# Attention's fixed order: new costs in its planner, four buffers for output halves, a split addition

## The chip, the cores and the metric

The kernel runs on one core of a Trainium2 chip. The metric is the device time of one execution in microseconds. Engines go by these names: PE is TensorE (matmuls and transposes), PEld its weight loads, DVE is VectorE, ACT is ScalarE, POOL is GpSimd, SP issues the DMAs. L12 is line 12 of the kernel before.

## The reference, cut to what matters

Three layers run one after the other: attention with queries pooled in pairs, a gated expert layer, and an expert layer with eight experts whose routing weights are normalised in eight rounds. Only attention's order is touched.

```python
q_pool = q.reshape(B, H, S // 2, 2, D).mean(axis=3)          # (2, 8, 576, 64)
scores = scale * np.matmul(q_pool, k.transpose(0, 1, 3, 2))  # (2, 8, 576, 1152)
scores = scores - np.max(scores, axis=-1, keepdims=True)
attn = np.exp(scores)
attn = attn / (np.sum(attn, axis=-1, keepdims=True) + 1e-09)
x = np.matmul(attn, v)                # then (1152, 512): tokens x heads * D
x = moe(x)                            # sigmoid(x @ w_gate) * (x @ w_val) @ w_out
out = moe2(x)                         # 8 experts, relu, weighted by P
```

## The kernel before, in words

**Attention.** The 16 heads are taken as eight pairs. A pair has nine units of up to 128 query rows: unit 0 holds the last 64 rows of both heads, units 1 to 4 are the other rows of the first head, 5 to 8 those of the second. Numbers are split in a high and a low part, so that a product is made of several fast ones.

For a unit `u`, PE computes the scores in three pieces (`scores`, L327/L328 for unit 0, L333/L334 for the others): columns 0 to 671 into the two banks of buffer A, columns 672 to 1151 into buffer B. There is one A and one B. DVE takes the negated maximum of A (`max_a`, step `ma`, L342) and of B (`max_b`, `mb`, L354) and the smaller of the two (`max_ab`, `m`, L360, one column). ACT takes the exponential of A with A's own maximum (`exp_a`, `ea`, L348; this frees A), that of B with the common one (`exp_b`, `eb`, L363; this frees B), and the factor between the two (`exp_ab`, `e`, L370). POOL multiplies A's part by this factor (`bring`, `b`, L374). PE transposes the unit in three groups (`turn_p`, `tpp`, L382) into PSUM buffers of kind "g", of which there are five. ACT copies the high part out (`p_high`, `ph`, L398) and DVE subtracts for the low part (`p_low`, `pl`, L402).

The product with the values runs in halves: for each head `j`, half `n` = 0 covers 256 rows, `n` = 1 covers 320. A half is 18 matmuls (`values`, `pv`, L421) into one "g" buffer. Its sums of exponentials are put together on POOL (`total`, `r1` and `r2`, L434). DVE adds 1e-9 (L439) and takes the reciprocal (L440), both in the step `r`, `reciprocals`; a half has two columns of sums, the half (0, 1) has three, since unit 0 is added. PE spreads the reciprocals (`turn_r`, `tr`, L445). ACT copies one part of the half out (`v_one`, `o1`, L457) into a buffer of kind "sw", DVE adds the other part (`o2`, L461) and multiplies by the reciprocals (`o3`, L466, L469), and POOL splits the result (`xh` at L71, `xl` at L477) into the input of the next layer. After `xl` the "sw" buffer is free; there are two.

Keys, queries and values of the next pairs are loaded by SP and prepared beside this (POOL: L71, L292, L262, L312; PE: L266, L296; ACT: L273, L302; DVE: L277).

**The planner.** Every such piece of work is a step with an engine, a due time `when`, an occupancy `takes` of its engine, a time `lasts` until its result is there (both in ns), the steps that it needs, and the buffers that it takes and frees. `arrange()` puts all steps in one order before the kernel is built. It keeps the time at which each engine is free, and again and again picks the step with the earliest possible start among those whose needs are placed and whose due time is at most `AHEAD` = 4 units past the oldest step not begun. A step on another engine than its producer may start `lasts + wake` after the producer's start, one on the same engine `takes` after it. On the chip each engine then runs its instructions in this order, each waiting for its real inputs.

**Behind attention.** The first expert layer's weights are split by `split_doubles` (L107 to L120). The first of these run on the same engine queues among the last steps of attention, by a rule of priority and not by the planner. The layer's matmuls are L712 to L714.

Of the kernel before, what the change touches and what calls it, by code (L numbers as in the profile page):

```python
# [8 lines left out]
F32 = mybir.dt.float32  # L9
# [20 lines left out]
def moe_stack_kernel(ctx: ExitStack, tc: tile.TileContext, q, k, v, wg1, wv1, wo1, wg2, w1, w2, out):  # L30
# [100 lines left out]
    with ExitStack() as pa:  # L131
# [6 lines left out]
        def slots(pool, n, shape, dt, name):  # L138
            return [pool.tile(shape, dt, tag=f"{name}{k}", name=f"{name}_{k}") for k in range(n)]
# [20 lines left out]

            "sum": slots(pw, 2, [P, 4, U], F32, "sum"),
            "rem": slots(pw, 1, [P, NJ, P], F32, "rem"),
            "sw": slots(pw, 2, [P, HALF[1][1]], F32, "sw"),
            "A": slots(ps_s, 1, [P, 2, 512], F32, "psA"),
            "B": slots(ps_s, 1, [P, 512], F32, "psB"),
            "g": slots(ps_s, 5, [P, 512], F32, "psg"),
# [2 lines left out]
        have = {}  # L169
        steps = {}  # L170

        def step(name, eng, when, takes, lasts, emit, deps=(), takes_buf=(), frees=()):


            steps[name] = dict(
                name=name, eng=eng, when=when, takes=takes, lasts=lasts, emit=emit, deps=deps, gets=takes_buf,
                frees=frees, seq=len(steps),
            )

        def arrange():  # L180

            wake = dict(PE=53, ACT=34, DVE=34, POOL=97, SP=100)
            users, need, ready = {}, {}, {e: [] for e in wake}
            for s in steps.values():
                need[s["name"]] = len(s["deps"])
                s["at"] = 0.0
                for d in s["deps"]:
                    users.setdefault(d, []).append(s)
                if not s["deps"]:
                    ready[s["eng"]].append(s)  # L190
            idle = {kind: [(0.0, k) for k in range(len(t))] for kind, t in stock.items()}
            line = sorted(steps.values(), key=lambda s: (s["when"], s["seq"]))
            turn = {kind: [s["name"] for s in line if any(k == kind for k, _ in s["gets"])] for kind in stock}
            given, front, free, out = {}, 0, dict.fromkeys(wake, 0.0), []
            begun = set()
            while len(out) < len(steps):
                while line[front]["name"] in begun or line[front]["eng"] == "SP":
                    front += 1
                limit, best = line[front]["when"] + AHEAD, None
                for eng, queue in ready.items():  # L200
                    for s in queue:
                        if s["when"] > limit and eng != "SP":
                            continue
                        t = max(free[eng], s["at"])
                        for kind, _ in s["gets"]:
                            if not idle[kind] or (kind != "g" and turn[kind][0] != s["name"]):
                                break
                            t = max(t, min(idle[kind])[0] + wake[eng])
                        else:
                            key = t, s["when"], s["seq"]  # L210
                            if best is None or key < best[0]:
                                best = key, s
                (t, _, _), s = best
                ready[s["eng"]].remove(s)
                begun.add(s["name"])
                free[s["eng"]] = t + s["takes"]
                for kind, what in s["gets"]:
                    slot = min(idle[kind])
                    idle[kind].remove(slot)
                    if kind != "g":  # L220
                        turn[kind].pop(0)
                    given[what] = kind, slot[1]
                s["got"] = [(what, *given[what]) for _, what in s["gets"]]
                for what in s["frees"]:
                    kind, k = given[what]
                    idle[kind].append((t + s["lasts"], k))
                for u in users.get(s["name"], ()):
                    own = s["takes"] if u["eng"] == s["eng"] else s["lasts"] + wake[u["eng"]]
                    u["at"] = max(u["at"], t + own)
                    need[u["name"]] -= 1  # L230
                    if not need[u["name"]]:
                        ready[u["eng"]].append(u)
                out.append((t, len(out), s))
            return [s for _, _, s in sorted(out, key=lambda x: x[:2])]
# [118 lines left out]
        def max_b(i, u):  # L353
            nc.vector.tensor_reduce(  # L354
                out=have["nm", i, u][:, 1:2], in_=have["B", i, u][:, 0:S - CA], axis=AX.X, op=ALU.max, negate=True
            )
# [54 lines left out]
        def rem_high(i, j):  # L411
            src, hi, _ = rem_parts(i, j)
            pool_copy(hi, src)
# [12 lines left out]
        def columns(j, n):  # L426
            c0 = 5 * j + 2 * n
            return slice(c0, c0 + 2 + (j == 0 and n == 1))
# [6 lines left out]

        def reciprocals(i, j, n):

            rs = have["sum", i][:, 3, columns(j, n)]
            nc.vector.tensor_scalar(out=rs, in0=rs, scalar1=eps, scalar2=None, op0=ALU.add)  # L439
            nc.vector.reciprocal(out=rs, in_=rs)  # L440

        def turn_r(i, j, n):
# [34 lines left out]
            nc.gpsimd.tensor_tensor(out=lo, in0=sw, in1=f(hi), op=ALU.subtract)  # L477

        def mm(w):
            return w / 2.4 + 13.4  # L480

        for i in range(B * NP):
            t0 = U * i
# [46 lines left out]
            for j in range(2):  # L530
# [9 lines left out]
                for g in range(3):  # L540
# [19 lines left out]
                )  # L560
                t = t0 + 4.5 + 4 * j
                step(
                    ("rh", i, j), "POOL", t, 637, 672, lambda i=i, j=j: rem_high(i, j),
                    [("rem", i, g) for g in range(3)] + [("ph", i, 3 + 4 * j, 0)],
                )
                step(
# [4 lines left out]
            for u in range(U):  # L571
                tu = t0 + order.index(u)
                js = (0, 1) if u == 0 else ((u - 1) // QT,)
                for g in range(3):
# [15 lines left out]
                )  # L590
                step(
                    ("ea", i, u), "ACT", ts + 0.01, 791, 822, lambda i=i, u=u: exp_a(i, u),
                    [("ma", i, u)] + [("ea", i, order[0])] * (u != order[0]),
                    [("p", ("p", i, u))] + ([("sum", ("sum", i))] if u == order[0] else []), [("A", i, u)],
                )
                step(("mb", i, u), "DVE", ts + 0.02, 564, 647, lambda i=i, u=u: max_b(i, u), [("s", i, u, 2), ("ma", i, u)])
                step(("m", i, u), "DVE", ts + 0.03, 130, 212, lambda i=i, u=u: max_ab(i, u), [("ma", i, u), ("mb", i, u)])
                step(
                    ("eb", i, u), "ACT", ts + 0.04, 632, 662, lambda i=i, u=u: exp_b(i, u), [("m", i, u), ("ea", i, u)],
                    [], [("B", i, u)],  # L600
                )
                step(("e", i, u), "ACT", ts + 0.05, 185, 283, lambda i=i, u=u: exp_ab(i, u), [("m", i, u), ("eb", i, u)], (), [("nm", i, u)])
                step(("b", i, u), "POOL", ts + 0.06, 789, 826, lambda i=i, u=u: bring(i, u), [("e", i, u), ("ea", i, u)])
                for g in range(3):
                    tp = tu + g / 3
# [4 lines left out]
                    if u == 0:  # L610
                        step(
                            ("rem", i, g), "ACT", tp + 0.001, 370, 490, lambda i=i, g=g: take_rem(i, g),
                            [("tpp", i, u, g)] + [("rem", i, 0)] * (g > 0), [("rem", ("rem", i))] if g == 0 else [], [("tpp", i, u, g)],
                        )
                        continue
                    j, n, tt = half_of(u)
                    step(
                        ("ph", i, u, g), "ACT", tp + 0.001, 370, 490, lambda i=i, u=u, g=g: p_high(i, u, g),
                        [("tpp", i, u, g)] + [("ph", i, u - tt, 0)] * (tt + g > 0),
                        [(f"pT{n}", ("pT", i, j, n))] if tt == 0 and g == 0 else [],  # L620
                    )
                    step(
                        ("pl", i, u, g), "DVE", tp + 0.002, 464, 547, lambda i=i, u=u, g=g: p_low(i, u, g),
# [4 lines left out]
            for j in range(2):  # L628
                for x, (n, jj, s) in enumerate((n, jj, s) for n in range(2) for jj in range(NJ) for s in range(2)):
# [1 line left out]
                    w, us = HALF[n][1], [1 + j * QT + 2 * n + tt for tt in range(2)]  # L631
                    end = jj == NJ - 1 and s == 1
                    step(
                        ("pv", i, j, n, jj, s), "PE", t, mm(w), w / 2.4 + 222,
                        lambda i=i, j=j, n=n, jj=jj, s=s: values(i, j, n, jj, s),
                        [("vl", i, j)] + [("pl", i, u, jj // 3) for u in us] + ([("rl", i, j)] if n else [])
                        + ([("pv", i, j, n, jj, 0)] if s else [("pv", i, j, n, jj - 1, 1)] if jj else []),
# [6 lines left out]
                    if (j, n) == (0, 1):  # L644
                        need += [("e", i, 0), ("eb", i, 0)]
                    step(
                        ("r1", i, j, n), "POOL", t - 0.5, 155, 195, lambda i=i, j=j, n=n: total(i, j, n, ALU.mult), need,
                    )
                    step(
                        ("r2", i, j, n), "POOL", t - 0.499, 155, 195, lambda i=i, j=j, n=n: total(i, j, n, ALU.add),  # L650
                        [("r1", i, j, n)],
                    )
                    step(
                        ("r", i, j, n), "DVE", t + 0.001, 230, 330, lambda i=i, j=j, n=n: reciprocals(i, j, n),
                        [("r2", i, j, n)],
                    )
                    step(
# [2 lines left out]
                        [("g", ("rb", i, j, n))], [("sum", i)] if j and n else [],  # L660
                    )
                    step(
                        ("o1", i, j, n), "ACT", t + 0.003, (400, 453)[n], (380, 435)[n],
                        lambda i=i, j=j, n=n: v_one(i, j, n), [("pv", i, j, n, jj, s)], [("sw", ("sw", i, j, n))],
                    )
                    step(
# [1 line left out]
                        lambda i=i, j=j, n=n: v_sum(i, j, n), [("o1", i, j, n)], [], [("pv", i, j, n)],  # L668
                    )
                    step(  # L670
                        ("o3", i, j, n), "DVE", t + 0.005, 331 + 131 * n, 416 + 131 * n,
                        lambda i=i, j=j, n=n: v_div(i, j, n), [("o2", i, j, n), ("tr", i, j, n)], [], [("rb", i, j, n)],
                    )
                    step(
# [420 lines left out]
```

## Time and profile before

| what | value |
|---|---|
| median of 3 runs | 1309.1 us (1308.77 to 1312.93) |
| the profiled execution | 1310.1 us, span of its instructions 1308.3 us |
| granted TensorE clock, mean | 0.998 of full speed |
| busy share of the span | PE 98%, PEld 90%, DVE 67%, ACT 42%, POOL 32% |
| attention | from 0 to about 302 us |

The profile is one execution. Busy time of an engine is the time in which an instruction of it runs; instructions of one engine may overlap a little, so that the next can start before the end of the last is recorded. Idle time is given with the event that ended it, which is inferred. Matmul ends are modelled.

### The profile page before, as it was taken

What the parts mean: (1) busy time and instruction counts of PE and PEld (TensorE: products, weight loads), DVE (VectorE), ACT (ScalarE), POOL (GpSimd) and SP (SyncE); (2) the same over time, 40 slices, a digit from 0 to 9 for tenths busy, and PEclk for the clock granted to TensorE, in tenths of its full rate; (3) what the DMA queues carried; (4) which work ended last, traced back from release to release, by engine and by line L of the source; (5) the groups of instructions that cost most, each with busy time, mean ns of one, the idle gap of its engine ahead of it and who ended that gap; (6) DMA issues with size and microseconds to landing.
All of it is one profiled execution on the core that took longest, in us unless ns stands there. A gap on an engine that the chain in (4) does not pass through costs nothing.

```text
span 1308.3 us, 20214 instructions
## 1 busy us (share of the span) xinstructions
PE 1277.9 (98%) x7770; PEld 1173.2 (90%) x7770; DVE 871.8 (67%) x1687; ACT 555.2 (42%) x1223; POOL 424.2 (32%) x495
## 2 busy tenths in 40 slices
PE   7899999998999999999999999999999999999998
PEld 5899898988999999889889989989988988998997
DVE  6998999997666664859557546646645745754643
ACT  7898898984333332523213213223312412421310
POOL 5788787665343433411102012012012102201000
PEclk9999999999999999999999999999999999999999
DMA  5111111112222332111012101111111210210001
GB/s 146 47 55 47 47 49 36 35 33 81 81 86 77 97 97 81 55 59 61 22 49 66 49 26 56 49 33 49 49 46 36 63 34 33 65 44 22 17 1 73
DMA packets 60863, 70.25 MB, mean 54 GB/s; under 512 B 3296, under 2 KB 47328, under 8 KB 60768
## 3 DMA queue, kind: packets, MB, share of 16 engines
q1 hardware_dynamic: 60768, 68.97, 17.1%
q8 instruction: 61, 1.00, 0.3%
q14 instruction: 34, 0.28, 0.1%
HBM read 66.60 MB, written 2.36 MB: 53 GB/s over the span
## 4 chain that ended last, share of the span: by engine, by line
PE 87%; DVE 9%; ACT 2%; issue 1%; DMA 1%; POOL 0%; DVEq 0%; ACTq 0%; POOLq 0%; SPq 0%
PE py L1048 10%; PE py L1049 10%; PE py L1050 10%; PE psb L714 8%; PE psb L712 8%; PE psb L713 7%; PE psg L421 4%; PE psg L382 4%; PE psa L712 2%; PE psa L714 2%; PE psc L712 2%; PE psa L713 2%; PE psc L714 2%; PE psc L713 2%; DVE pT L402 2%; PE pso L712 2%
## 5 line engine op out<-in xcount | busy, mean ns | idle before, releaser
L930 POOL TENSOR_TENSOR sm_w<-raw_w 128x256 f32<-128x256 f32 x64 | 55.3, 865 | 590.8 <-issue 529.9
L1048 PE MATMUL py<-wsp_w,ht 128*128 128x512 f32 x576 | 227.8, 396 | 0.0
L1049 PE MATMUL py<-wsp_w,ht 128*128 128x512 f32 x576 | 227.8, 395 | 0.0
L1050 PE MATMUL py<-wsp_w,ht 128*128 128x512 f32 x576 | 227.8, 395 | 0.0
L1061 DVE SCALAR_TENSOR_TENSOR acc<-py,pr,acc 128x512 f32<-128x512 f32 x126 | 94.4, 749 | 191.8 <-PE py L1050 191.8
L78 ACT ACTIVATE wsp_w<-raw_w 128x1024 fp32r<-128x1024 f32 x32 | 34.0, 1061 | 312.4 <-PE py L1050 274.3
L421 PE MATMUL psg<-pT,vs 128*128 128x256 f32 (+1 forms) x576 | 147.9, 324 | 0.9 <-DVE pT L402 0.8
L1050 PEld LDWEIGHTS py<-wsp_w,ht 128*128 128x128 f32 x576 | 108.3, 188 | 26.2
L1048 PEld LDWEIGHTS py<-wsp_w,ht 128*128 128x128 f32 x576 | 108.3, 188 | 25.4
L1049 PEld LDWEIGHTS py<-wsp_w,ht 128*128 128x128 f32 x576 | 108.3, 188 | 25.4
L382 PE MATMUL psg<-ident,p 128*128 128x128 f32 x648 | 105.7, 273 | 4.5 <-DVE pT L402 3.2
L402 DVE TENSOR_TENSOR pT<-psg,pT 128x384 fp32r<-128x384 f32 x192 | 101.3, 548 | 5.2 <-ACT pT L398 3.8
L984 ACT ACTIVATE ht<-pw 128x576 fp32r<-128x576 f32 x96 | 65.3, 683 | 89.7 <-DVE pw L974 89.6
L714 PE MATMUL psb<-x,w_gv 128*128 128x384 f32 x288 | 97.1, 337 | 3.5 <-POOL w_gv L120 3.5
L421 PEld LDWEIGHTS psg<-pT,vs 128*128 128x128 f32 x576 | 95.2, 189 | 4.5 <-DVE pT L402 1.0
L712 PE MATMUL psb<-x,w_gv 128*128 128x384 f32 x288 | 96.9, 336 | 0.0
L713 PE MATMUL psb<-x,w_gv 128*128 128x384 f32 x288 | 96.8, 336 | 0.0
L974 DVE TENSOR_TENSOR pw<-psb,pw 128x288 f32<-128x288 f32 x192 | 85.6, 451 | 14.5 <-PE psb L714 13.5
L398 ACT ACTIVATE pT<-psg 128x384 fp32r<-128x384 f32 x192 | 90.4, 491 | 7.7 <-PE psg L382 4.4
L382 PEld LDWEIGHTS psg<-ident,p 128*128 128x128 f32 x648 | 79.4, 140 | 10.2 <-POOL sum L434 2.6
L985 DVE SCALAR_TENSOR_TENSOR ht<-pw,ht 128x576 fp32r<-128x576 f32 x96 | 72.8, 759 | 11.2 <-ACT ht L984 10.7
L712 PE MATMUL psb<-xc,w_w 128*128 128x288 f32 x256 | 75.7, 296 | 1.0 <-DVE pw L974 1.0
(205 smaller groups left out, 3381.9 us busy)
## 6 DMA issues: line engine op xcount, KB each, us to landing
raw_w<-in_moe_w_dram SPq DMA_DIRECT2D x64, 512.0 KB, 3.6
raw_gv<-in_moe_w_gate_dram SPq DMA_DIRECT2D x12, 512.0 KB, 3.5
raw_gv<-in_moe_w_val_dram SPq DMA_DIRECT2D x12, 512.0 KB, 3.6
raw_o<-in_moe_w_out_dram SPq DMA_DIRECT2D x12, 512.0 KB, 3.4
kr<-in_k_dram SPq DMA_DIRECT2D x16, 288.0 KB, 3.1
vr<-in_v_dram SPq DMA_DIRECT2D x16, 288.0 KB, 2.8
qr<-in_q_dram SPq DMA_DIRECT2D x16, 256.0 KB, 3.3
out_dram<-acc SPq DMA_DIRECT2D x9, 256.0 KB, 2.0
```

Source lines behind the costliest of these rows:

```text
L382: nc.tensor.transpose(have["tpp", i, u, g][:, n * P:(n + 1) * P], have["p", i, u][:, jj * P:(jj + 1) * P], ident)
L398: nc.scalar.activation(out=p_parts(i, u, g)[0], in_=turned(i, u, g), func=AF.Copy)
L402: nc.vector.tensor_tensor(out=lo, in0=turned(i, u, g), in1=f(hi), op=ALU.subtract)
L421: nc.tensor.matmul(have["pv", i, j, n][:, 0:HALF[n][1]], have["vs", i, j][:, jj].rearrange("p a d -> p (a d)"), have["pT", i, j, n][s][:, ...
L712: nc.tensor.matmul(ps, wh, xh, start=first, stop=False, skip_group_check=more)
L713: nc.tensor.matmul(ps, wh, xl, start=False, stop=False, skip_group_check=more)
L714: return nc.tensor.matmul(ps, wl, xh, start=False, stop=last, skip_group_check=more).ins
L974: ins = nc.vector.tensor_tensor(out=out_[:, cols], in0=ps[key][nb][:, 0:HB], in1=in_[:, cols], op=ALU.add).ins
L1048: nc.tensor.matmul(py, hh, wr[:, 0], start=(x == 0), stop=False)
L1049: nc.tensor.matmul(py, hh, wr[:, 1], start=False, stop=False)
L1050: nc.tensor.matmul(py, hl, wr[:, 0], start=False, stop=(x == 3))
L1061: nc.vector.scalar_tensor_tensor(out=acc[t], in0=py, scalar=pr[:, t, e:e + 1], in1=acc[t], op0=ALU.mult, op1=ALU.add)
```

## The change

Three things change, all inside attention.

1. `step` gets a list `after`: needs that are only an order on the same engine, not a result. Needs on a result count as `lasts + wake`, on the same engine too, except on PE and POOL; needs in `after` count as `takes`. Many needs of ACT (and `mb` behind `ma` on DVE) move to `after`. The wake times grow, and the costs of the matmuls over 400 columns and of the steps `rh`, `pv`, `r1`, `r`, `o1` and `o3` get other values.
2. The kind "sw" gets four buffers in place of two.
3. The addition of 1e-9 to three columns becomes one instruction for two columns and one for the third.

```diff
-            "sw": slots(pw, 2, [P, HALF[1][1]], F32, "sw"),
+            "sw": slots(pw, 4, [P, HALF[1][1]], F32, "sw"),
...
-        def step(name, eng, when, takes, lasts, emit, deps=(), takes_buf=(), frees=()):
+        def step(name, eng, when, takes, lasts, emit, deps=(), takes_buf=(), frees=(), after=()):
...
-                name=name, eng=eng, when=when, takes=takes, lasts=lasts, emit=emit, deps=deps, gets=takes_buf,
-                frees=frees, seq=len(steps),
+                name=name, eng=eng, when=when, takes=takes, lasts=lasts, emit=emit, deps=(*deps, *after),
+                after=after, gets=takes_buf, frees=frees, seq=len(steps),
...
-            wake = dict(PE=53, ACT=34, DVE=34, POOL=97, SP=100)
+            wake = dict(PE=145, ACT=80, DVE=40, POOL=140, SP=100)
...
-                    own = s["takes"] if u["eng"] == s["eng"] else s["lasts"] + wake[u["eng"]]
+                    own = s["lasts"] + wake[u["eng"]]
+                    if s["name"] in u["after"] or u["eng"] == s["eng"] in ("PE", "POOL"):
+                        own = s["takes"]
...
-            rs = have["sum", i][:, 3, columns(j, n)]
-            nc.vector.tensor_scalar(out=rs, in0=rs, scalar1=eps, scalar2=None, op0=ALU.add)
+            c = columns(j, n)
+            rs = have["sum", i][:, 3, c]
+            for part in (rs[:, 0:2], rs[:, 2:c.stop - c.start])[0:c.stop - c.start - 1]:
+                nc.vector.tensor_scalar(out=part, in0=part, scalar1=eps, scalar2=None, op0=ALU.add)
             nc.vector.reciprocal(out=rs, in_=rs)
...
-            return w / 2.4 + 13.4
+            return w / 2.4 + (17 if w > 400 else 13.4)
...
-                    ("rh", i, j), "POOL", t, 637, 672, lambda i=i, j=j: rem_high(i, j),
+                    ("rh", i, j), "POOL", t, 752, 672, lambda i=i, j=j: rem_high(i, j),
...
-                    [("ma", i, u)] + [("ea", i, order[0])] * (u != order[0]),
+                    [("ma", i, u)],
...
+                    after=[("ea", i, order[0])] * (u != order[0]),
...
-                step(("mb", i, u), "DVE", ts + 0.02, 564, 647, lambda i=i, u=u: max_b(i, u), [("s", i, u, 2), ("ma", i, u)])
+                step(("mb", i, u), "DVE", ts + 0.02, 564, 647, lambda i=i, u=u: max_b(i, u), [("s", i, u, 2)], after=[("ma", i, u)])
...
-                    ("eb", i, u), "ACT", ts + 0.04, 632, 662, lambda i=i, u=u: exp_b(i, u), [("m", i, u), ("ea", i, u)],
-                    [], [("B", i, u)],
+                    ("eb", i, u), "ACT", ts + 0.04, 632, 662, lambda i=i, u=u: exp_b(i, u), [("m", i, u)], [], [("B", i, u)],
+                    after=[("ea", i, u)],
...
-                        ("pv", i, j, n, jj, s), "PE", t, mm(w), w / 2.4 + 222,
+                        ("pv", i, j, n, jj, s), "PE", t, mm(w), w / 2.4 + 300,
...
-                        ("r1", i, j, n), "POOL", t - 0.5, 155, 195, lambda i=i, j=j, n=n: total(i, j, n, ALU.mult), need,
+                        ("r1", i, j, n), "POOL", t - 0.5, 275, 195, lambda i=i, j=j, n=n: total(i, j, n, ALU.mult), need,
...
-                        ("r", i, j, n), "DVE", t + 0.001, 230, 330, lambda i=i, j=j, n=n: reciprocals(i, j, n),
+                        ("r", i, j, n), "DVE", t + 0.001, 570 if (j, n) == (0, 1) else 400, 650 if (j, n) == (0, 1) else 480, lambda i=i, j=j, n=n: reciprocals(i, j, n),
...
-                        ("o1", i, j, n), "ACT", t + 0.003, (400, 453)[n], (380, 435)[n],
+                        ("o1", i, j, n), "ACT", t + 0.003, (550, 600)[n], (530, 585)[n],
...
-                        ("o3", i, j, n), "DVE", t + 0.005, 331 + 131 * n, 416 + 131 * n,
+                        ("o3", i, j, n), "DVE", t + 0.005, 460 + 131 * n, 546 + 131 * n,
```

In the same way the need of `e` on `eb`, those of `rem` on its first group and those of `ph` on the first group of its half move to `after`.

## Rows read from the trace of the kernel before

**Rows 1.** The page's line of engines: busy us, share of the span, instructions.

```profile
PE 1277.9 (98%) x7770; PEld 1173.2 (90%) x7770; DVE 871.8 (67%) x1687; ACT 555.2 (42%) x1223; POOL 424.2 (32%) x495
```

**Rows 2.** Windows: length, each engine's busy us (instructions), granted clock, DMA share, GB/s.

```profile
20.00:60.00 40.00, 35.34 (x241) 30.70 (x240) 35.12 (x73) 34.47 (x97) 29.75 (x39) 1.00 0.23 66
60.00:260.00 200.00, 195.11 (x1407) 182.00 (x1406) 183.70 (x408) 180.44 (x480) 155.61 (x215) 1.00 0.16 44
260.00:302.10 42.10, 38.96 (x282) 36.40 (x281) 38.06 (x88) 32.64 (x85) 29.07 (x43) 1.00 0.08 26
...
306.30:532.00 225.70, 225.70 (x1293) 225.70 (x1294) 139.07 (x203) 79.93 (x110) 89.45 (x59) 0.99 0.28 87
```

**Rows 3.** Waits, 0 to 302 us: who waited for whom, us, times, longest.

```profile
PEld psA L333 <- ACT p L348: 7.0, 12, 1.5
...
ACT p L363 <- DVE nm L360: 5.8, 18, 0.9
```

**Rows 4.** Chain that ended last, 109.8 to 121 us: start, us, what.

```profile
113.24 0.21 DVE nm L360
113.45 0.93 DVE pT L402 x2
...
115.16 0.66 DVE sum L439
...
115.84 0.18 DVE sum L440
...
117.06 0.21 DVE nm L360
...
119.44 0.92 ACT p L348 x2
...
120.41 0.42 PE psA L333
```

**Rows 5.** Timeline (start, us, instruction), and one group by form (busy, mean ns | idle).

```profile
44.77 2.62 DVE L439 TENSOR_SCALAR sum<-sum,eps 128x3 f32<-128x3 f32 x1
...
44.80 2.38 POOL L262 TENSOR_TENSOR qs<-qr 128x1024 f32<-128x1024 f32 x1
...
118.51 0.84 DVE L342 TENSOR_REDUCE nm<-psA 128x1 f32<-128x672 f32 x1
...
281.88 1.17 DVE L439 TENSOR_SCALAR sum<-sum,eps 128x2 f32<-128x2 f32 x1
...
281.61 1.42 POOL L312 TENSOR_TENSOR vs<-vr,vs 128x576 fp32r<-128x576 f32 x1
...
L439 DVE TENSOR_SCALAR sum<-sum,eps 128x3 f32<-128x3 f32 x8 | 6.6, 825 | 0.3 <-POOL sum L434 0.2
```

**Rows 6.** Timeline of DVE, 280 to 290 us.

```profile
280.14 0.64 DVE L354 TENSOR_REDUCE nm<-psB 128x1 f32<-128x480 f32 x1
280.82 0.21 DVE L360 TENSOR_SCALAR nm<-nm 128x1 f32<-128x1 f32 x1
280.95 1.01 DVE L402 TENSOR_TENSOR pT<-psg,pT 128x384 fp32r<-128x384 f32 x2
...
289.19 0.64 DVE L354 TENSOR_REDUCE nm<-psB 128x1 f32<-128x480 f32 x1
289.75 0.67 DVE L109 SCALAR_TENSOR_TENSOR dv_gv<-dv_gv,ds_gv 128x512 int32<-128x512 int32 x1
```

**Rows 7.** Tile sw (ns min/median/max, first and last start); timeline of PE and POOL.

```profile
L457 ACT ACTIVATE sw<-psg x32: 375/405/437, 39.8 to 302.1; 64x256 f32<-64x256 f32 x16, 64x320 f32<-64x320 f32 x16
...
299.16 2.88 PE L421 MATMUL psg<-pT,vs 128*128 128x320 f32 x18
...
299.36 0.87 POOL L477 TENSOR_TENSOR x<-sw,x 64x320 fp32r<-64x320 f32 x1
```

**Rows 8.** Timeline of PE and DVE behind attention, idle time in brackets.

```profile
306.24 0.69 PE L714 MATMUL psb<-x,w_gv 128*128 128x384 f32 x1 [3.51 <-POOL w_gv L120]
...
302.59 0.50 DVE L461 TENSOR_TENSOR sw<-psg,sw 64x320 f32<-64x320 f32 x1 [1.23 <-ACT sw L457]
```

More of the change, by code (lines that the diff above doesn't have):

```diff
@@ L592, in moe_stack_kernel @@
                     ("ea", i, u), "ACT", ts + 0.01, 791, 822, lambda i=i, u=u: exp_a(i, u),
-                    [("ma", i, u)] + [("ea", i, order[0])] * (u != order[0]),
+                    [("ma", i, u)],
                     [("p", ("p", i, u))] + ([("sum", ("sum", i))] if u == order[0] else []), [("A", i, u)],
+                    after=[("ea", i, order[0])] * (u != order[0]),
                 )
-                step(("mb", i, u), "DVE", ts + 0.02, 564, 647, lambda i=i, u=u: max_b(i, u), [("s", i, u, 2), ("ma", i, u)])
+                step(("mb", i, u), "DVE", ts + 0.02, 564, 647, lambda i=i, u=u: max_b(i, u), [("s", i, u, 2)], after=[("ma", i, u)])
                 step(("m", i, u), "DVE", ts + 0.03, 130, 212, lambda i=i, u=u: max_ab(i, u), [("ma", i, u), ("mb", i, u)])
                 step(
-                    ("eb", i, u), "ACT", ts + 0.04, 632, 662, lambda i=i, u=u: exp_b(i, u), [("m", i, u), ("ea", i, u)],
-                    [], [("B", i, u)],
-                )
-                step(("e", i, u), "ACT", ts + 0.05, 185, 283, lambda i=i, u=u: exp_ab(i, u), [("m", i, u), ("eb", i, u)], (), [("nm", i, u)])
+                    ("eb", i, u), "ACT", ts + 0.04, 632, 662, lambda i=i, u=u: exp_b(i, u), [("m", i, u)], [], [("B", i, u)],
+                    after=[("ea", i, u)],
+                )
+                step(
+                    ("e", i, u), "ACT", ts + 0.05, 185, 283, lambda i=i, u=u: exp_ab(i, u), [("m", i, u)], (), [("nm", i, u)],
+                    after=[("eb", i, u)],
+                )
                 step(("b", i, u), "POOL", ts + 0.06, 789, 826, lambda i=i, u=u: bring(i, u), [("e", i, u), ("ea", i, u)])
@@ L612, in moe_stack_kernel @@
                             ("rem", i, g), "ACT", tp + 0.001, 370, 490, lambda i=i, g=g: take_rem(i, g),
-                            [("tpp", i, u, g)] + [("rem", i, 0)] * (g > 0), [("rem", ("rem", i))] if g == 0 else [], [("tpp", i, u, g)],
+                            [("tpp", i, u, g)], [("rem", ("rem", i))] if g == 0 else [], [("tpp", i, u, g)],
+                            after=[("rem", i, 0)] * (g > 0),
                         )
@@ L618, in moe_stack_kernel @@
                         ("ph", i, u, g), "ACT", tp + 0.001, 370, 490, lambda i=i, u=u, g=g: p_high(i, u, g),
-                        [("tpp", i, u, g)] + [("ph", i, u - tt, 0)] * (tt + g > 0),
-                        [(f"pT{n}", ("pT", i, j, n))] if tt == 0 and g == 0 else [],
+                        [("tpp", i, u, g)], [(f"pT{n}", ("pT", i, j, n))] if tt == 0 and g == 0 else [],
+                        after=[("ph", i, u - tt, 0)] * (tt + g > 0),
                     )
```

## The prediction

> **What bounds the kernel now.** I read the page's line of engines first: over the whole span TensorE (PE) is busy 98% and VectorE (DVE) 67% [rows 1]. A figure of the whole hides the stage that is touched, so next came the windows. Attention, the only stage with a planner, ends at 302.1 us; from 306.3 to 532 us the first expert layer runs PE for 225.70 of 225.70 us [rows 2]. Nothing of the change is in that part, so what attention ends earlier or later goes whole into the total.
>
> Inside attention PE sat idle 4.66 us between 20 and 60, 4.89 between 60 and 260 (200 - 195.11) and 3.14 between 260 and 302.1, together 12.7 us, and 3.51 more before the third product of the expert layer [rows 2, 8]. DVE is nearly as full, 183.70 of 200 us in the steady part [rows 2]. So two engines run close to full and each waits for the other now and then. The waits say where: PE waited 7.0 us with weight loads for the first exponential (L348), which frees the only score buffer A, and L363 waited 5.8 us for the small minimum L360 [rows 3].
>
> The chain shows one such stretch, from 113.2 to 120.4 us, nearly all DVE: the minimum L360, then L402 and L342, the addition L439 for 0.66 us, the reciprocal L440, L402 and L354 again, and the next L360 [rows 4]. The chain's last DVE step is hidden behind a POOL name: the maximum L342 runs from 118.51 for 0.84 us, and L348 starts at 119.44, 0.09 us after it ends [rows 4, 5]. From L348's start PE needs 0.97 us to its next score matmul (119.44 to 120.41) [rows 4].
>
> **What the planner believes and the trace says.** The order is fixed in advance, so a wrong cost does harm only by a wrong order. Three errors are in that stretch. The minimum L360 starts 0.68 us after L354 starts (280.14 to 280.82), because it needs L354's result; an unrelated operation started after 0.56 (289.19 to 289.75) [rows 6]. The old planner puts 564 ns on both; the new one 647 + 40 = 687 ns on the first. From L348's start to the next scores it has 822 + 53 = 875 ns and gets 822 + 145 = 967, which is the trace's 0.97. And the step with L439 has 230 ns where the chain takes 0.66 + 0.02 + 0.18 = 0.86; it gets 570. These three move towards the trace. One moves away: the copy L457 takes 375 to 437 ns [rows 7], its old occupancies are 400 and 453 ns, the new ones 550 and 600.
>
> **The change part by part.**
>
> *New delays and occupancies.* No instruction is added or removed, only the order on the four engines moves, and no row of before shows the new order. Bounds: the most it can give is PE's whole idle time between 20 and 302.1, 12.7 us; the most I allow it to cost is the wait for buffer A once more, 7.0 us [rows 3]. My value lies between. Of the 3.14 us at the end I count nothing: the last pair has no later work to fill in. Of the 4.89 us in the steady part I count half, 2.4: in the stretch above the unseen cost is 2 x 0.12 for L360 behind L354, 0.86 - 0.23 = 0.63 for the addition and 0.09 before the scores, together 0.96 us; but only what another ready instruction can cover goes, and of these parts the addition (0.63) is work of DVE that stays, wherever it is put. Of the 4.66 us before 60 I count two thirds, 3.1, because one order alone weighs there: L439 sat on DVE for 2.62 us from 44.77 while the POOL addition L262 ran from 44.80 for 2.38 [rows 5]. Together 5.5 us less.
>
> [...] The rows have the unrelated operation start 0.12 us sooner behind L354 than the dependent one [rows 6]. [...]
>
> *The split addition.* Eight steps (one in each pair of heads) issue one more DVE instruction. What does L439 wait for? The three-column form has a mean of 825 ns in 8 [rows 5]. But at 281.88 a two-column one took 1.17 us and ended (283.05) as the POOL operation L312 ended (281.61 + 1.42 = 283.03), just as the three-column one at 44.77 ended 0.2 us behind L262. So both shapes wait for a running POOL operation. The first part of the split keeps two columns, so the wait stays, and the second part is added: L360, also of one column, takes 0.21 us and lets the next start 0.13 us behind it (280.82 to 280.95) [rows 6]. Eight such are 1.0 us on DVE. Ends: 1.0 us more if all lie on the path, and 8 x (825 - 210 - 130) = 3.9 us less if the three columns were the cause after all. I take 0.8 us more, six of eight: in the stretch of rows 4 the chain passes through this step, and where it doesn't, PE's queue of transposes and products hides it.
>
> *Four buffers for output halves.* A half takes its buffer at the copy L457 and frees it behind L477. The 32 copies lie (302.1 - 39.8) / 31 = 8.5 us apart on average, so two buffers come round every 17 us. They are closest at the end: the last L457 follows the last 18 products, which run from 299.16 for 2.88 us, to 302.04, and its buffer was freed by L477 at 299.36 + 0.87 = 300.23 [rows 7]. It waited for PE and not for a buffer, with 1.8 us to spare; So 0; the ends are 0.4 us (one copy's length) either way, if the freer choice moves a copy in the order.
>
> *What ends last afterwards.* PE at 306.24 waits for L120, the low part of the first expert weights [rows 8]. Its DVE inputs queue behind L461 at 302.59, which waited 1.23 us for the last copy. These instructions are no part of the plan, yet share its queues; where they fall among the new order I can't derive. I leave the 3.51 us as they are; they may go wholly or grow by one DVE step of 0.7 us.
>
> Sum on the profiled execution's 1310.1 us (span 1308.3 and 1.8 around it): 1310.1 - 5.5 + 0.8 = 1305.4. That execution lies 1.0 above the median of the runs, 1309.1, so the prediction is 1304.4.
>
> **Rivals.**
>
> *The order changes and the time doesn't (rival 1).* PE is at work in 195.11 of 200 us of the steady part; a stall that is filled in one unit comes back in the next, because there is still one buffer A. For it: the idle time that can be had at all is small there. Against it: the stalls sit in a few long stretches, not spread out. Time: 1309.1 + 0.8 for the split = 1309.9. A smaller form of it: the gaps before L360 cannot be filled. Then a quarter of the unseen cost, 0.24 of 0.96, stays, and with it a quarter of 5.5, 1.4 us: 1305.8, inside the bound; it has 0.03 of this rival's chance, since the rows speak against it [rows 6]. [...]
>
> *The planner fills the gap with something too long (rival 2, slower).* It picks the earliest start; with L360's step 123 ns later, a ready L402 (half of the chain's 0.93 for two at 113.45, 0.46 us) goes in between, and L360 comes 0.46 - 0.12 = 0.34 us later than now. Behind L360 wait L363, L370 and POOL's scaling L374, then the transposes on PE. It decides where ACT has nothing else ready: L363 waited for L360 in 18 places already. 18 x 0.34 = 6.1 us on the path: 1309.1 + 6.1 = 1315.2; with a fifth of it hidden, 1314.0. For it also speaks L457's overcharge. Against it: the saved 0.12 us of DVE is spent on work that is due anyway.
>
> *The split removes the wait (rival 3).* Then 3.9 us less instead of 0.8 more: 1304.4 - 4.7 = 1299.7. Against it: the two-column row above.
>
> **How the numbers follow.** About 0.3%, or 3.9 us, is what a measurement of this kernel can tell from no change: below 1305.2 is faster, above 1313.0 slower. The forecast (a gain of 4 to 10 us) gets 0.40 and rival 3 0.04, both faster: 0.44. Rival 1 gets 0.34, all within the bound. Rival 2 gets 0.22, slower. For 8 in 10 the low end is 12.7 us below the median, all of PE's idle time, 1296.4, taken as 1297; the high end takes in the part of rival 2 in which a fifth is hidden, 1314. The forecast's own range is 1299 to 1305.2.
>
> **What would show it.** Right: PE's idle time falls between 20 and 260, the wait of PE's loads for L348 drops below 7.0 us, more L354 are followed by L402 and not by L360, while the two-column part of the split still stretches to the end of a POOL operation. Wrong: those waits stay or grow; or L363's wait for L360 rises over 5.8 us (rival 2); or no addition exceeds 0.25 us (rival 3). The four buffers would show as wrong if L457 starts sooner behind its last product than the 0.09 us at the end. The prediction fails altogether if the stretch between 302.1 and 306.3 changes by more than attention itself.

## The result and the profile after

The changed kernel takes 1297.74 us in the median of four runs (1296.58 to 1298.43), beside 1309.62 for the kernel before on the same chip: ratio 0.9904, interval 0.9884 to 0.9923. That is 11.9 us less by the medians. Forecast were 1304.4 us and a range of 1297 to 1314: direction and range held, the gain is over twice the 4.7 to 5.2 us of the sum. The profiled execution took 1298.43 us with a span of 1296.3, 12.0 less than before. Lines of the changed kernel are 2 to 9 higher: L342 is now L344, L348 L350, L354 L356, L360 L362, L363 L365, L402 L404, L421 L423, L439 L443, L457 L461, L477 L481.

The windows of the changed kernel; columns as in [rows 2], and beside PE's busy time stands its count of matmuls:

```profile
20.00:60.00 40.00, 38.13 (x277) 35.44 (x278) 36.29 (x82) 37.74 (x106) 31.93 (x43) 1.00 0.23 68
60.00:260.00 200.00, 196.75 (x1456) 186.62 (x1455) 187.87 (x425) 182.96 (x495) 163.12 (x224) 1.00 0.15 44
```

Between 60 and 260 us PE's idle time fell from 4.89 to 3.25 us, which is 1.64. But PE did 1456 matmuls where it had done 1407 [rows 2]; at 200 / 1456 = 0.137 us each the 49 more are worth 6.7 us. So in this stretch most of the gain was not in the idle time. The whole of attention, to the end of its last products, shows both parts, first before, then after:

```profile
0.00:302.10 302.10, 282.19 (x1999) 259.73 (x2000) 268.14 (x584) 260.00 (x686) 224.98 (x312) 1.00 0.19 53
```

```profile
0.00:289.40 289.40, 275.35 (x2000) 257.88 (x2001) 262.67 (x592) 256.00 (x686) 223.49 (x311) 1.00 0.19 56
```

PE's idle time is 302.10 - 282.19 = 19.91 us before and 289.40 - 275.35 = 14.05 after, which is 5.9 less; its busy time for the same work, to within one matmul, is 6.8 less. How can the same work be busy for less time? Records of neighbouring matmuls overlap (576 products of 0.321 us on average fill only 135.6 us), so a matmul that comes a little late need not leave a gap. That this is where the 6.8 us sat is inferred, and which matmuls came sooner was not followed.

The waits of the changed kernel that answer to [rows 3]:

```profile
ACT p L365 <- DVE nm L362: 8.9, 16, 0.7
...
PEld psA L335 <- ACT p L350: 3.0, 4, 1.5
```

PE's loads wait 3.0 us for the exponential that frees buffer A, not 7.0. L365 waits longer for the small minimum, 8.9 us and not 5.8. Why that is so stands in the timeline of DVE:

```profile
141.96 0.65 DVE L356 TENSOR_REDUCE nm<-psB 128x1 f32<-128x480 f32 x1
142.52 0.54 DVE L404 TENSOR_TENSOR pT<-psg,pT 128x384 fp32r<-128x384 f32 x1
142.98 0.20 DVE L362 TENSOR_SCALAR nm<-nm 128x1 f32<-128x1 f32 x1
143.10 1.01 DVE L404 TENSOR_TENSOR pT<-psg,pT 128x384 fp32r<-128x384 f32 x2
```

An L404 starts 0.56 us behind L356, in the gap that stood open in [rows 6] (0.68 to the dependent L360). L362 comes later by the 0.46 us of that L404 less the gap, and DVE loses nothing. Counted over the timeline of DVE, L362 follows L356 at once in 12 of 72 places, before in 50; in 30 an L404 stands first.

A second pair of dependent steps came apart in the same way. The multiplication L466 (now L470) needs the sum L461 (now L465); it followed at once in 30 of 32 halves before and does so in 1 now. The idle time of DVE ahead of the small minimum and of this multiplication is the last number of each row, first before, then after:

```profile
L360 DVE TENSOR_SCALAR nm<-nm 128x1 f32<-128x1 f32 x72 | 15.2, 211 | 1.8
L466 DVE TENSOR_TENSOR sw<-psg,sw 64x256 f32<-64x256 f32 x31 | 13.1, 422 | 3.1 <-PE psg L296 0.5
```

```profile
L362 DVE TENSOR_SCALAR nm<-nm 128x1 f32<-128x1 f32 x72 | 14.5, 202 | 0.5
L470 DVE TENSOR_TENSOR sw<-psg,sw 64x256 f32<-64x256 f32 x32 | 13.3, 415 | 0.6
```

In some stretches the chain is PE's own now, where [rows 4] had DVE:

```profile
145.53 0.22 PE psB L330
145.74 0.43 PE psg L423 x3
146.18 0.33 PE psg L384 x3
146.51 0.15 PE psg L423
146.65 0.15 PE psA L335
```

That does not hold of the whole. Between 60 and 260 us the products L423 stand in the chain with 13.9%, before with 20.4%, and L404 with 10.9%, before with 7.6%: DVE is still on it.

The addition that had lasted 2.62 us beside L262 in [rows 5] now runs elsewhere, at 41.50, beside the end of another POOL operation; its first part and the column added behind it together take 0.50 us. Behind attention the first expert weights make PE wait as long as before (3.51 us in [rows 8]), only 12.7 us earlier:

```profile
41.50 0.50 DVE L443 TENSOR_SCALAR sum<-sum,eps 128x2 f32<-128x2 f32 x2
```

```profile
293.54 0.69 PE L723 MATMUL psb<-x,w_gv 128*128 128x384 f32 x1 [3.52 <-POOL w_gv L120]
```

### The profile page after: what moved, and what is told of

Its sections match the earlier page's. It is cut to its first block, busy times and chain, and to the rows that moved or that the text cites. A ratio compares the mean times of both kernels' runs of the same rounds, so it can differ in the third digit from the quotient of the medians.

```text
span 1296.3 us, 20186 instructions
## 1 busy us (share of the span) xinstructions
PE 1272.1 (98%) x7770; PEld 1172.5 (90%) x7770; DVE 867.2 (67%) x1695; ACT 551.6 (43%) x1223; POOL 423.5 (33%) x495
## 4 chain that ended last, share of the span: by engine, by line
PE 84%; DVE 9%; ACT 4%; issue 1%; DMA 1%; POOL 1%; SPq 0%; ACTq 0%; POOLq 0%; DVEq 0%
PE py L1057 10%; PE py L1059 10%; PE py L1058 10%; PE psb L723 8%; PE psb L721 8%; PE psb L722 8%; PE psg L423 3%; PE psc L721 3%; PE psa L721 3%; DVE pT L404 3%; PE psc L723 3%; PE psc L722 3%; PE psa L723 3%; PE psa L722 2%; PE psg L384 2%; PE pso L723 2%
## 5 line engine op out<-in xcount | busy, mean ns | idle before, releaser
L423 PE MATMUL psg<-pT,vs 128*128 128x256 f32 (+1 forms) x576 | 135.6, 321 | 0.9 <-DVE pT L404 0.7
L404 DVE TENSOR_TENSOR pT<-psg,pT 128x384 fp32r<-128x384 f32 x192 | 102.7, 549 | 6.9 <-ACT pT L400 5.4
L423 PEld LDWEIGHTS psg<-pT,vs 128*128 128x128 f32 x576 | 92.0, 189 | 5.1 <-DVE pT L404 1.4
```

The lines of the kernel that those rows point to most:

```text
L404: nc.vector.tensor_tensor(out=lo, in0=turned(i, u, g), in1=f(hi), op=ALU.subtract)
L423: nc.tensor.matmul(have["pv", i, j, n][:, 0:HALF[n][1]], have["vs", i, j][:, jj].rearrange("p a d -> p (a d)"), have["pT", i, j, n][s][:, ...
```

## The experiments

Theory A: the gain comes from truer costs, above all from the rule that lets the planner see DVE's own gap and fill it. Theory B: any new order is a draw, and this one is a lucky draw. Beside them the prediction's terms for the split and the buffers were at stake. Every ratio is to the kernel before on the same chip. The expected times start from 1309.6 us for the kernel before; on the chips of these runs it took 1311.0 to 1312.0, so the difference by the ratio is the better comparison. "At once" counts the maxima L354 (of 72) that the small minimum follows at once, and the sums L461 (of 32) that the multiplication follows at once. The last column takes attention by the ends of its products: when the first pair of heads ends, how long the six pairs behind it take, and how long the last, in us.

| kernel | ratio (interval) | at once, L354 | at once, L461 | first, six, last |
|---|---|---|---|---|
| before | 1 | 50 | 30 | 71.8, 209.0, 21.3 |
| changed | 0.9904 (0.9884 to 0.9923) | 12 | 1 | 66.8, 202.9, 19.6 |
| same-engine rule alone | 0.9934 (0.992 to 0.9949) | 17 | 2 | 67.7, 208.2, 19.1 |
| wake times alone | 0.9994 (0.9985 to 1.0004) | 50 | 29 | 72.7, 210.5, 20.4 |
| occupancies alone | 0.9967 (0.9954 to 0.998) | 52 | 30 | 70.7, 206.0, 22.3 |
| wake times and rule | 0.9918 (0.9901 to 0.9934) | 32 | 1 | 67.3, 206.7, 18.4 |
| changed, rule undone | 0.9975 (0.9963 to 0.9987) | 57 | 27 | 70.2, 207.2, 22.9 |
| changed, costs 10% untrue | 0.9952 (0.9938 to 0.9967) | 21 | 4 | 76.0, 203.3, 18.7 |
| changed, old costs of the copy | 0.9906 (0.9891 to 0.9921) | 14 | 1 | 66.9, 205.6, 19.9 |

**The parts of the planner, one at a time, on the kernel before.**

```diff
-                    own = s["takes"] if u["eng"] == s["eng"] else s["lasts"] + wake[u["eng"]]
+                    own = s["lasts"] + wake[u["eng"]]
+                    if s["name"] in u["after"] or u["eng"] == s["eng"] in ("PE", "POOL"):
+                        own = s["takes"]
```

The lists `after`, which keep mere orders out of this rule, are part of this edit.

> The kernel before, with one part of the change: a need on a result counts lasts + wake on DVE and ACT too (old wakes 34, old occupancies, two buffers, one addition). Theory A (the planner now sees that L360 must wait for L354, and fills the gap): this part alone brings about half of the 11.9 us, so 1302 to 1305, and of 72 L354 at most 25 are followed by L360 at once instead of 50. Theory B (any new order is a draw, the costs' truth does not matter): anything between 1297 and 1316, no tie to the gaps filled.

Measured 1302.56 us beside 1311.9: 8.7 us less by the ratio, about two thirds of the gain. Theory A's time and count both held, and the share is more than its half. PE's rows of this kernel:

```profile
0.00:294.90 294.90, 282.75 (x1999) 259.10 (x2000) 263.93 (x584) 259.19 (x686) 225.36 (x312) 1.00 0.19 55
...
60.00:260.00 200.00, 198.78 (x1424) 183.92 (x1424) 185.50 (x413) 181.96 (x484) 160.58 (x221) 1.00 0.15 44
```

Over the whole of attention its PE is idle for 12.15 us, 7.8 less than before, and busy for 0.6 more: what the rule gains alone is idle time. Between 60 and 260 us its PE is idle for only 1.22 us, less than in the changed kernel, and yet it does 32 matmuls fewer: idle time doesn't order these two.

The rule also charges L466 for its need of L461. DVE's idle time before L466 falls from 3.1 us to 0.7 with the rule alone, before L360 from 1.8 to 0.8. No run takes one of the two gaps by itself, so how the 8.7 us divide between them is open. Nor is it the steady part that gains: 4.1 us come by the end of the first pair, 2.2 in the last, and 0.8 in the six between, though gaps are filled in all.

```diff
-            wake = dict(PE=53, ACT=34, DVE=34, POOL=97, SP=100)
+            wake = dict(PE=145, ACT=80, DVE=40, POOL=140, SP=100)
```

> The kernel before with the new wake times alone (PE 145, ACT 80, DVE 40, POOL 140). Theory A: PE's waits for buffer A fall, 3 to 5 us less, 1304 to 1307; L354 is still followed by L360 in 45 or more places. Theory B: anything between 1297 and 1316.

Measured 1310.51 beside 1311.9; the interval holds 1. A miss for theory A: truer delays between engines alone bring nothing that shows, though the wait of PE's loads for buffer A falls from 7.0 to 5.3 us. In this order one three-column addition lasts 3.56 us, from 43.86, longer than any before; but its six pairs take 1.5 us more than before too.

```diff
-            return w / 2.4 + 13.4
+            return w / 2.4 + (17 if w > 400 else 13.4)
...
-                        ("r", i, j, n), "DVE", t + 0.001, 230, 330, lambda i=i, j=j, n=n: reciprocals(i, j, n),
+                        ("r", i, j, n), "DVE", t + 0.001, 570 if (j, n) == (0, 1) else 400, 650 if (j, n) == (0, 1) else 480, lambda i=i, j=j, n=n: reciprocals(i, j, n),
...
```

> The kernel before with the new occupancies alone (matmuls over 400 columns, rh, pv, r1, r, o1, o3). Theory A: small, 0 to 3 us less, 1306.5 to 1310, since o1 moves away from its trace. Theory B: anything between 1297 and 1316.

Measured 1307.04 beside 1311.9: inside the expected times, but 4.3 us less by the ratio where 0 to 3 were expected, and this with no gap filled (52 and 30 at once).

Wake times and rule together (both edits above):

> The kernel before with the new wake times and the same-engine rule, old occupancies. Theory A: nearly all of the gain, 1298 to 1301. Theory B: no sum of the two parts; anything between 1297 and 1316.

Measured 1300.61 beside 1311.9, 10.8 us less, inside theory A's times. Against the rule alone that is 2 us more. The intervals of the ratios overlap, but on this one chip all four times (1300.17 to 1301.14) lie below all four of the rule alone (1302.03 to 1304.06), so that the wake times add something to the rule is likely. Fewer gaps behind L354 are filled than with the rule alone (32 at once, not 17): the count doesn't order these two.

**The rule taken out of the changed kernel.**

```diff
-                    if s["name"] in u["after"] or u["eng"] == s["eng"] in ("PE", "POOL"):
+                    if u["eng"] == s["eng"]:
                         own = s["takes"]
```

> The changed kernel with the same-engine rule undone (a need on the same engine counts takes again), all else new. Theory A: the largest part goes, 1303 to 1308, and L354 is followed by L362 at once in 45 or more of 72 places. Theory B: 1297 to 1316.

Measured 1308.94 beside 1312.01. The time is 0.9 us above theory A's; by the ratios 3.3 us of gain are left, some 9 of 12.6 are gone, and the count is back at 57. Put in alone the rule brings 8.7, taken out it costs 9: both sides agree, which theory B doesn't give. Here 4.3 of it is lost in the six pairs, so beside the other new costs the rule does help there.

**Costs made untrue.**

```diff
+            kind = str((name[0] if isinstance(name, tuple) else name, eng))
+            takes, lasts = (x * (0.9 + 0.2 * (zlib.crc32(f"{kind}{z}1".encode()) % 1000) / 999) for z, x in enumerate((takes, lasts)))
             steps[name] = dict(
```

> The changed kernel with every occupancy and duration in the plan multiplied by its own factor between 0.9 and 1.1, fixed for each kind of step: costs made 10% untrue at most, another order in half of all places. Theory A (truth of the costs): some of the gain is lost, 1300 to 1306, but the time stays below that of before. Theory B (the changed kernel's order is a lucky draw among many): 1305 to 1315.

Measured 1306.23 beside 1312.01, half of the gain. The time lies 0.2 us above theory A's and inside theory B's. By the ratio it is 6.3 us less (4.3 to 8.1), inside what theory A allows from 1309.6 (3.6 to 9.6 less) and mostly above theory B's most (4.6). So this run alone decides little. Where the loss lies says more: the six pairs take 203.3 us, nearly as in the changed kernel (202.9), and all of the loss is in the first pair, 76.0 and not 66.8. Its start differs: PE stood idle for 3.83 us before 19.99, and the granted clock from 20 to 40 us was 0.86 of full speed, a part of it at 1.2 and not 2.4 GHz, where the changed kernel has 1.00. This one set of errors cost several us, but not in the steady part.

**The copy's costs.**

```diff
-                        ("o1", i, j, n), "ACT", t + 0.003, (550, 600)[n], (530, 585)[n],
+                        ("o1", i, j, n), "ACT", t + 0.003, (400, 453)[n], (380, 435)[n],
```

> The changed kernel with the copy's costs as before (400 and 453 ns, nearer to the 375 to 437 ns of the trace). Theory A taken strictly: 0 to 2 us faster than the changed kernel. If the higher value stands for something true that the duration does not show (the copy's start behind PE and DVE's wait for it): 1 to 4 us slower.

Measured 1300.43 beside 1312.01, ratio 0.9906 (0.9891 to 0.9921): the same as the changed kernel. The one cost that moved away from the trace neither helps nor harms by more than the 2 us of the interval. In the profile the last products end at 292.5 us, 3.1 later than in the changed kernel, so a loss of this size from the old costs is not ruled out.

**The split addition.** Alone on the kernel before, with the order as it was:

```diff
-            nc.vector.tensor_scalar(out=rs, in0=rs, scalar1=eps, scalar2=None, op0=ALU.add)
+            for part in (rs[:, 0:2], rs[:, 2:c.stop - c.start])[0:c.stop - c.start - 1]:
+                nc.vector.tensor_scalar(out=part, in0=part, scalar1=eps, scalar2=None, op0=ALU.add)
```

> The kernel before with the split alone, order unchanged. By the prediction 0.8 us slower than before (0 to 1.0); if three columns were the cause of the wait, 3.9 us faster.

Measured 1312.36 beside 1311.02, ratio 1.0013 (1.0004 to 1.0022): slower by 1.7 us (0.5 to 2.9), somewhat more than expected. In the profiles the last products of attention end at 302.9 us, 0.9 later than before. DVE and then POOL in this kernel, at the place of [rows 5]:

```profile
44.71 2.77 DVE L443 TENSOR_SCALAR sum<-sum,eps 128x2 f32<-128x2 f32 x2
47.52 0.17 DVE L444 RECIPROCAL sum<-sum 128x3 f32<-128x3 f32 x1
```

```profile
44.76 2.40 POOL L264 TENSOR_TENSOR qs<-qr 128x1024 f32<-128x1024 f32 x1
```

The two-column part waits for POOL just as three columns did, and the third column comes on top.

The changed kernel with one instruction again (the edit above undone):

> The changed kernel with the three-column addition in one instruction again; plan and order are the same, eight DVE instructions fewer. If both shapes wait for a running POOL operation (the prediction): 0 to 1.0 us faster than the changed kernel (1296.7 to 1297.7 where that has 1297.7), each three-column addition as long as the two-column part was. If three columns were the cause: 2 to 4 us slower, with additions of 0.8 us.

Measured 1297.9 beside 1311.02, ratio 0.9895 (0.9881 to 0.9908). From the end of the first half's products to the last it takes 249.8 us in its profile and in that of the changed kernel: in the new order the split costs nothing that shows. Its eight three-column additions last as long as the two-column parts did, within 0.05 us.

Every addition column by column:

```diff
-            for part in (rs[:, 0:2], rs[:, 2:c.stop - c.start])[0:c.stop - c.start - 1]:
+            for x in range(c.stop - c.start):
+                part = rs[:, x:x + 1]
```

> The changed kernel with every addition of 1e-9 done column by column (two or three instructions of one column each), same plan and order. If one column never waits for POOL: all 72 take 0.20 to 0.23 us, also those beside a POOL operation, and the eight that lasted 0.37 to 0.94 us are gone: DVE gains about 8 x 0.3 us and loses 24 x 0.13 us, so 0 to 2 us faster in total. If the wait has to do with the moment and not with the shape, some one-column additions last over 0.3 us and the time is 0 to 2 us slower.

Measured 1297.26 beside 1311.02, ratio 0.9891 (0.9877 to 0.9904). The additions in this kernel (least, median and most ns):

```profile
L444 DVE TENSOR_SCALAR sum<-sum,eps x72: 187/203/215, 29.4 to 285.3; 128x1 f32<-128x1 f32 x72
```

None of 72 waits, and 29 of them end while a POOL operation goes on. (The changed kernel had 13 two-column additions of 0.37 to 0.94 us, not the eight of the expectation.) At 111.13 three of them run, 0.44 us in all, while POOL's L482 runs from 111.04 to 111.78:

```profile
111.13 0.44 DVE L444 TENSOR_SCALAR sum<-sum,eps 128x1 f32<-128x1 f32 x3
```

```profile
111.04 0.74 POOL L482 TENSOR_TENSOR x<-sw,x 64x256 fp32r<-64x256 f32 x1
```

So the shape decides: one column passes, two and three wait. By the same measure as above (249.2 us) it gains 0.6 us, less than the timed runs can tell.

**Two buffers for output halves.**

```diff
-            "sw": slots(pw, 4, [P, HALF[1][1]], F32, "sw"),
+            "sw": slots(pw, 2, [P, HALF[1][1]], F32, "sw"),
```

> The changed kernel with two buffers for output halves again. The plan comes out the same, and in the trace of the changed kernel never more than two such buffers are in use at once: by the prediction no difference (within 1 us). If the buffers matter, a copy L461 waits for POOL's last subtraction and the time is 1 to 5 us longer.

Measured 1298.02 beside 1311.02, ratio 0.9895 (0.9881 to 0.9908), the last products end at 289.4 us and not 289.3. The buffers do nothing.

**A version that points further:** one-column additions, and `AHEAD = 3.0`.

> The changed kernel with one-column additions only and AHEAD = 3.0 in place of 4.0, for which the planner's own end of attention is 278.8 instead of 280.2 us. Theory A: now that its costs are close, its difference of 1.4 us shows on the chip within 2 us: 1294.5 to 1298. Theory B: 1290 to 1310, no tie to the plan.

Measured 1295.16 beside 1312.01, ratio 0.9869 (0.9852 to 0.9885). It is the fastest of all and lies in theory A's times. By the ratio it is 4.6 us below the changed kernel, more than the planner's 1.4; but its interval touches those of the changed kernel and of one-column additions alone, so that it beats these is not shown.

## Why the prediction was right or wrong

**Direction: right, and in part for the reason given.** The gap behind L354 is filled, PE's loads wait less for buffer A, and the rule alone carries about two thirds of the gain. But the rule fills a second gap, that between L461 and L466, which the prediction didn't see, and what the filled gaps gain without the other new costs lies mostly in the first and the last pair. The Trainium skill, "VectorE: DVE Perf Modes", section "The DRAIN you can't avoid", says that the next operation waits until the pipeline is empty, and adds that one that is not held starts earlier. The trace agrees with the second: at 142.52 L404 starts 0.09 us before the recorded end of L356.

**Size: the order's term was too small.** The step that failed is "the most it can give is PE's whole idle time", with half of 4.89 us counted for the steady part. PE's idle time in attention fell by 5.9 us, close to the 5.5 counted; the other 6.8 came out of time that the profile calls busy, and for that the sum had nothing. That the 5.9 came so near is luck in part: idle time fell by 2.8 us from 20 to 60 where 3.1 were counted, by 1.6 from 60 to 260 where 2.4 were, and from 260 on by 2.2 where nothing was, while in the first 20 us it rose by 0.7. By the ends of the products the first pair of heads gained 71.8 - 66.8 = 5.0 us, the six pairs behind it 6.0, and the last pair 1.7, together 12.7; in this profile the layers behind take 0.7 us longer, so that 12.0 are left of it. Counting nothing for the last pair was wrong by its own ground too, though which of its instructions moved was not followed. Why PE's busy time fell is open: with the rule alone it didn't, nor with the wake times or the occupancies alone.

**The other costs.** The 0.09 us before the scores is what the wake times correct, and alone they bring nothing. The occupancies bring 4.3 us alone; which of them was not separated, except that in the changed kernel the copy's show no effect in the times.

**The split: right.** 0.8 us forecast in the old order, 0.9 by the profiles and 1.7 (0.5 to 2.9) by the times, and the wait is by POOL and not by three columns; in the new order even this is gone.

**The buffers: right,** nothing. **What ends last afterwards: right,** the 3.5 us behind attention stayed.

**Rivals.** Rival 1 fell with the time, and its smaller form with the gaps that were filled. Rival 2's mechanism is there, an L404 ahead of the small minimum in 30 places and L365's wait up to 8.9 us, but not its price: naming that wait as a sign of a slower kernel was a mistake, since the kernel is faster with it. Rival 3 fell with the two-column part at 44.71.

**Left open.** How much of the 12 us is luck of this order: only one set of untrue costs was run; it kept half, and what it lost lay in the first pair. Open too is which of the two filled gaps did more.

## What to carry to other kernels

Where an order is planned from costs, the wait of an engine on its own last result is a cost like any other: with it in the plan, two pairs of dependent steps came apart, with other work between them, and that brought 8.7 us of 1311.9. To judge what a stage gained, take the time between the same two events of its work, as the ends of the first and the last products. Idle time of a pipelined engine gave 5.9 us of 12.7 here. A count of matmuls in a fixed window misleads as well: between 60 and 260 us it is 1447 with the untrue costs and 1424 with the rule alone, which gains more. So does the busy time of one group: that of the products falls from 147.9 to 139.3 us with the wake times alone, which gain nothing.

## What the runs showed of the hardware

A DVE addition of a scalar to two or three columns waits until the POOL operation running beside it ends (2.62 us for three columns, 1.17 for two); to one column none waited (72 of 72 between 187 and 215 ns). A DVE operation that needs the result of the one before starts later than one that doesn't: behind a maximum over 128x480 it started after 0.68 us [rows 6], an unrelated one after 0.56 (at 142.52).
